# Softcap attention and a two-way maxout: six subtractions of the weights on one engine, and a new order of all work

## The chip, the cores and the metric

The kernel runs on one core of one Trainium2 chip. A core has a matrix engine (TensorE, PE in the profile; its weight loads are PEld), a vector engine (VectorE, DVE), a scalar engine for tanh and exp (ScalarE, ACT), a general engine (GpSimd, POOL) and a queue engine (SyncE, SP). Each takes its own instructions in order. Transfers between the outer memory and the core run on 16 DMA engines and are issued from the queues of POOL, SP and ACT. The metric is the time of one execution on the device, in microseconds (us), as the median over several runs: 332.95 us before the change (three runs, 332.04 to 333.63). All times within an execution count from the start of the span.

## What is computed

Attention over 8 batches of 12 heads, 448 positions and 64 channels, with a soft cap on the scores; its output, as 3584 rows of 768, goes through two weight matrices, an elementwise maximum and an output matrix:

```python
scores = scale * np.matmul(q, k.transpose(0, 1, 3, 2))
scores = cap * np.tanh(scores / cap)
attn = np.exp(scores - max); attn = attn / (sum + 1e-09)
x = np.matmul(attn, v)            # heads side by side: 3584 x 768
g = np.maximum(x @ w1, x @ w2)    # w1, w2: 768 x 1024
out = g @ w_out                   # 1024 x 768
```

(The lines are shortened from the reference.) Inputs and output are float32.

## The kernel before

**The second part, rewritten.** Since max(a, b) = relu(a - b) + b, the kernel computes out = relu(x (w1 - w2)) w_out + x (w2 w_out). Two things are made once at the start: `wd_sb` = w1 - w2, in six chunks c = 0..5 of 128 rows, and `wm_sb` = w2 w_out. The first needs one subtraction for each chunk: a float32 chunk of w1 (512 KB) and a bf16 chunk of w2, 128 partitions by 1024, written as bf16:

```python
def subtract(c, eng):
    eng.tensor_sub(wd_sb[:, c, :], w1_in[c], w2b[:, c, :])
```

`eng` is DVE or POOL. For `wm_sb` TensorE turns each w2 chunk (`W`, then `WC` copies it out), multiplies it with w_out in two halves of 8 matmuls (`P`; `OP` opens the PSUM bank) and DVE keeps the result (`PC`, line 389), which frees the bank.

**Staging of the weights.** The w2 chunks lie in the memory that later holds gT; w1 chunks 0 to 3 lie in the four output buffers `osb`, 4 and 5 in a buffer of `xT`. All these loads (`lw1`, `lw2`, `lwo`) and all loads of k, q and v (`lk`, `lq`, `lv`) are issued from POOL's queue, in order. A load into a buffer waits until its last readers are through.

**The first part.** It runs over 48 pairs of heads i, two of which make a tile t (24 tiles). For i < 10 TensorE turns q and k (`X i bank`, 28 small matmuls; DVE copies them out with `XC`); for later tiles an SP transpose by DMA does it (`cr t`). `S i j` are the scores of key chunk j (3 chunks of 128 keys), `T` their tanh and `E` their exp on ACT; `L`, `TL`, `EL` do the same for the last 64 keys of a tile. `A` and `B` add exps on DVE (for t >= 3), `Y` sums them on TensorE, `Y1` to `Y3` turn, invert and spread the sums on DVE. `VL` and `V` multiply with v, and `N t u` normalizes on DVE into `xT`. Scores and values share two PSUM tiles, `s0` and `s1`: a step that opens one of them waits for the one that read it last (`S 7 2`, for instance, waits for both `N 2`). DVE does `N t 1` in two instructions of half the partitions.

**The second part's main loop.** 120 groups: per batch 8 of x (w1 - w2) (columns 448 wide) and 6 or 8 of the output (384 wide). `M x y n` issues n pairs of half-array matmuls, the upper half of the rows for group x beside the lower half for group y; -1 means no partner, and `M x x` uses the whole array. `O` opens a PSUM bank, `H` and `Hs` hand a bank's accumulation from one half to the other over a marker instruction on DVE or SP, `ev` (DVE) or `eva` (ACT) evacuates, `st` stores by SP.

**What sets the order.** Nothing in the program chooses an order: the string `ORDER` (lines 9 to 166) lists every step of the whole kernel, and the steps are called in turn. Each step appends its instructions to the queue of its engine; engines run on their own and wait for one another by semaphores. So two steps of different engines may swap places in the string without effect, while two of the same engine change that engine's queue. Warm-up matmuls without use (`D`) keep TensorE busy in the beginning. The lines of the profile: `subtract` 354, `keep_wm` 389, `transposes` 410, `keep_warm` 423, `scores` 466, `tanh` 471, `left` 480, `ex` 488, `add` 500 and 505, `total` 518 to 525, `invert` 530 to 536, `values_left` 552, `values` 558, `normalize` 570 and 573, pairs of the main loop 597 (592 for the whole array), evacuation 622, 656, 658 and 661.

In the order before, POOL has `sub 5 1` (the 1 means POOL) between `lv 3 0` and `lv 3 1`; the other five are on DVE as 0, 2, 1, 3, 4.

Of the kernel before, what the change touches and what calls it, by code (L numbers as in the profile page):

```python
# [9 lines left out]
ld0 k; ld0 q; ms0; dm; cd k; lk 1 0; lq 1 0; lw2 3; lk 2 0; lw2 2; id; lq 3 0; lq 2 0; lw2 0; lw2 1; lk 3 0;  # L10
D 3 16; cd q; D 3 15; Xh 0 0 0; Xh 0 1; D 3 4; XCh 0 0; XCh 0 1; D 3 4; S 0 0; D 3 5; S 0 1; D 3 4; T 0 0; T 0 1;
D 3 4; S 0 2; D 3 12; X 1 1; D 3 16; W 3 2; XC 1; ms; WC 3; L 0; T 0 2; E 0 0 3; TL 0; S 1 2; D 3 8; X 2 2; S 1 0;
D 3 8; W 2 0; D 3 4; T 1 2; T 1 0; S 1 1; E 1 2 3; T 1 1; XC 2; S 2 1; D 3 1; W 1 3; X 3 2; S 2 0; W 0 1; lk 4 0;
lq 4 0; lwo 0 0; lwo 0 1; lv 0 0; lv 0 1; lk 6 0; lwo 1 0; lwo 1 1; lq 5 0; lv 1 1; lk 7 0; lq 6 0; lk 5 0; lw2 5;
lq 7 0; lv 1 0; T 2 1; T 2 0; WC 1; XC 3; WC 2; WC 0; L 1; X 4 2; S 2 2; OP 2 0 0; P 2 0 1; OP 1 0 1; P 1 0 3;
OP 0 0 3; P 0 0 2; P 1 0 1; P 0 0 1; P 2 0 1; P 0 0 1; P 2 0 2; P 1 0 1; P 2 0 3; P 1 0 3; P 2 0 1; TL 1; EL 0;
T 2 2; EL 1; E 1 0 2; XC 4; PC 2 0; PC 1 0; S 3 0; VL 0; V 0 1 0 2; Y 0 0; V 0 0 0 3; V 0 1 2 3; Y1 0; Y2 0; Y3 0;
N 0 1; N 0 0; T 3 0; E 2 0 3; S 3 1; OP 2 1 2; P 2 1 2; OP 1 1 0; P 1 1 1; OP 0 1 1; P 0 1 1; P 0 0 1; P 1 1 2;
P 0 1 3; P 0 0 2; P 2 1 2; P 1 1 1; P 0 0 1; S 3 2; T 3 1; E 3 0 2; T 3 2; S 4 0; P 0 1 2; P 1 1 2; P 0 1 2;
P 2 1 3; P 1 1 1; S 4 1; T 4 0; E 3 2 3; T 4 1; PC 0 1; PC 0 0; S 4 2; X 5 1; OP 3 0 3; P 3 0 2; P 2 1 1; P 1 1 1;  # L20
XC 5; PC 2 1; PC 1 1; L 2; W 5 1; T 4 2; TL 2; VL 1; V 1 0 0 1; Y 1 0; V 1 0 1 3; V 1 1 0 3; S 5 0; Y1 1; Y2 1;
WC 5; Y3 1; lv 2 1; lw2 4; lk 8 0; lq 9 0; lq 8 0; lw1 0; lw1 2; lk 9 0; lv 2 0; E 4 0 3; T 5 0; X 6 0; XC 6;
N 1 0; N 1 1; P 3 0 3; S 5 1; OP 3 1 2; P 3 1 1; W 4 0; P 3 0 3; P 3 1 7; S 5 2; EL 2; T 5 1; E 5 0 2; T 5 2;
WC 4; PC 3 1; PC 3 0; sub 0 0; S 6 0; OP 4 0 0; P 4 0 8; X 7 3; S 6 1; PC 4 0; XC 7; sub 2 0; T 6 0; E 5 2 3;
T 6 1; S 6 2; X 8 2; X 9 0; L 3; T 6 2; TL 3; Y 2 3; VL 2; S 7 0; V 2 1 0 1; EL 3; T 7 0; XC 8; XC 9; Y1 2; lw1 1;
lw1 5; lk 10 1; lw1 3; lw1 4; lk 12 1; lk 10 0; lq 11 0; lv 3 0; sub 5 1; lv 3 1; lk 11 0; lk 11 1; lq 10 0;
V 2 1 1 2; V 2 0 0 3; V 2 1 2 3; OP 5 0 3; P 5 0 1; OP 4 1 0; P 4 1 2; OP 5 1 2; P 5 1 1; S 7 1; P 4 1 2; P 5 1 3;
P 4 1 1; P 5 1 1; P 5 0 4; P 4 1 1; P 5 0 3; P 5 1 3; P 4 1 2; E 6 0 3; T 7 1; Y2 2; Y3 2; sub 1 0; N 2 1; N 2 0;
sub 3 0; PC 5 0; PC 5 1; sub 4 0; S 7 2; S 8 0; E 7 0 2; T 7 2; T 8 0; O 0 1; M 0 -1 1; O 1 3; M 1 -1 2; M 0 -1 3;
S 8 1; M 0 -1 2; M 1 -1 1; S 8 2; Hs 0; cr 5; T 8 1; T 8 2; E 7 2 3; M 1 0 3; O 2 2; M 2 0 3; L 4; VL 3; A 3 1 1;  # L30
A 3 0 1; A 3 0 2; B 3 0; B 3 1; PC 4 1; A 3 1 2; TL 4; V 3 0 0 3; V 3 1 0 3; Y 3 0; S 9 0; M 2 1 3; ev 0; Y1 3;
Hs 2; EL 4; T 9 0; E 8 0 3; O 3 0; M 3 1 3; M 3 2 3; Hs 3; lv 4 1; lv 4 0; lq 12 0; lv 5 0; lk 13 0; lk 13 1;
lk 12 0; lq 13 0; lk 15 0; lv 6 3; lv 5 2; lk 14 1; lk 15 1; lq 14 0; lk 14 0; lv 5 3; lq 15 0; lv 5 1; S 9 1;
O 4 1; M 4 2 3; M 4 3 3; Y2 3; Y3 3; ev 1; N 3 0; ev 2; T 9 1; Hs 4; O 5 3; M 5 3 3; M 5 4 3; O 6 2; M 6 4 3;
ev 3; N 3 1; A 4 0 1; ev 4; Hs 5; M 6 5 3; O 7 0; M 7 5 2; S 10 0; Hs 6; M 7 5 1; M 7 6 1; S 9 2; M 7 6 2; Hs 7;
cr 6; E 9 0 2; T 10 0; T 9 2; E 9 2 3; O 8 1; M 8 6 3; S 10 2; M 8 7 3; S 10 1; A 4 1 1; ev 5; A 4 0 2; H 8;
B 4 1; B 4 0; A 4 1 2; ev 6; T 10 1; T 10 2; O 9 3; M 9 7 3; M 9 8 5; L 5; M 9 8 2; VL 4; V 4 1 0 2; Y 4 2;
V 4 0 0 3; V 4 1 2 3; TL 5; E 10 0 3; ev 7; Y1 4; Y2 4; Y3 4; N 4 1; N 4 0; S 11 0; M 9 8 4; O 10 0; M 10 8 3;
Hs 9; Hs 8 2; T 11 0; EL 5; M 10 9 3; M 8 9 2; S 11 1; M 8 9 4; S 11 2; M 8 9 2; O 11 2; M 11 9 1; T 11 1; T 11 2;
E 11 0 2; M 11 9 2; S 12 0; M 11 10 5; S 12 1; M 11 10 6; T 12 1; T 12 0; E 11 2 3; A 5 0 1; ev 8; O 12 1;  # L40
M 12 10 3; cr 7; Hs 11; H 10 2; A 5 1 1; ev 9; A 5 0 2; B 5 1; B 5 0; M 12 11 3; M 10 11 1; L 6; M 10 11 2;
S 12 2; M 10 11 5; ev 10; A 5 1 2; TL 6; T 12 2; O 13 3; M 13 11 3; S 13 0; M 13 12 4; VL 5; Y 5 0; V 5 1 0 3;
V 5 0 0 3; T 13 0; E 12 0 3; M 13 12 4; S 13 1; M 13 12 3; lv 6 0; lk 17 0; lv 6 1; lk 16 0; lk 17 1; lv 7 0;
lv 7 3; lq 16 0; lq 17 0; lk 16 1; lk 19 1; lv 6 2; Y1 5; Y2 5; Y3 5; N 5 0; N 5 1; ev 11; T 13 1; EL 6; E 13 0 2;
Hs 13; O 14 0; M 14 12 3; M 14 13 1; S 14 0; M 14 13 2; Hs 12 2; Hs 14; S 13 2; M 12 13 8; O 15 2; M 15 13 3;
# [12 lines left out]
S 18 0; M 24 25 4; O 27 2; M 27 25 3; M 27 26 5; S 18 1; T 18 0; E 17 2 3; T 18 1; M 27 26 1; S 18 2; M 27 26 5;
L 9; A 8 0 1; A 8 0 2; ev 24; A 8 1 1; B 8 1; B 8 0; A 8 1 2; ev 25; T 18 2; TL 9; O 28 1; M 28 26 3; VL 8;
V 8 0 0 1; Y 8 3; V 8 1 0 3; V 8 0 1 3; S 19 0; M 28 27 3; E 18 0 3; T 19 0; Y1 8; cr 10; st 1 3; Hs 26 2; Hs 28;  # L60
M 26 27 8; O 29 3; M 29 27 3; S 19 1; EL 9; T 19 1; Y2 8; Y3 8; N 8 0; N 8 1; A 9 0 1; ev 26; A 9 0 2; ev 27;
S 19 2; M 29 28 8; S 20 0; M 29 28 3; O 30 0; M 30 28 3; Hs 29; Hs 28 2; lk 23 0; lk 22 0; lq 23 0; lk 23 1;
lk 22 1; lq 22 0; lv 9 3; lv 9 1; M 30 29 3; T 19 2; E 19 0 2; T 20 0; E 19 2 3; Hs 30; cr 11; M 28 29 8; S 20 1;
O 31 2; M 31 29 3; S 20 2; M 31 30 3; A 9 1 1; B 9 1; ev 28; ev 29; B 9 0; H 31; A 9 1 2; T 20 1; T 20 2; O 32 1;
M 32 30 3; M 32 31 3; Y 9 3; L 10; VL 9; V 9 1 0 2; V 9 0 0 3; V 9 1 2 3; E 20 0 3; TL 10; ev 30; Y1 9; Y2 9;
Y3 9; st 1 6; Hs 32; O 33 0; M 33 31 3; M 33 32 2; S 21 0; M 33 32 1; O 34 3; M 34 32 3; EL 10; T 21 0; N 9 0;
N 9 1; ev 31; ev 32; Hs 33; lk 25 0; lq 25 0; lv 10 0; lv 10 1; lk 25 1; lk 24 1; lv 11 0; lk 24 0; lq 24 0;
lv 10 2; lv 10 3; lk 26 1; lv 11 3; S 21 2; M 34 33 3; S 21 1; O 35 2; M 35 33 3; Hs 34; st 1 5; T 21 2; T 21 1;
E 21 0 2; M 35 34 3; Hs 35; O 36 1; M 36 34 3; M 36 35 3; S 22 1; S 22 0; ev 33; ev 34; A 10 0 1; A 10 0 2; Hs 36;
# [665 lines left out]
```

## Time and profile before

| | |
|---|---|
| median of three runs | 332.95 us (332.04 to 333.63) |
| the profiled execution | 335.05 us, its span 333.3 us |
| mean granted TensorE clock | 0.992 |
| TensorE busy | 325.7 us (98%) |
| ScalarE busy | 284.4 us (85%) |
| VectorE busy | 240.1 us (72%) |
| GpSimd busy | 164.8 us (49%) |
| TensorE's share of the chain that ended last | 84% |
| subtractions (line 354) on VectorE, of 1.21 to 3.17 us | 5 |
| subtraction on GpSimd, 2.14 us | 1 |

The page gives for each engine the busy time and its share of the span, a strip of 40 slices (each 8.3 us) with the busy share in tenths, and the chain: the work that ended last, followed back step by step to what released it. Rows of instructions name a line, an engine, an operation, and the tile written from the tile read. A row of waits says who waited for whom, with the total, the number of times and the longest. Busy time on TensorE counts from a matmul's start to its modelled end; pairs on the two halves of the array overlap, so sums of durations exceed the time.

### The profile page before, as it was taken

How to read it: one execution, taken by the hardware profiler on the slowest of the kernel's cores; microseconds unless marked ns; L12 is line 12 of the kernel's file. 1: busy time of each engine (PE TensorE's matmuls, PEld its weight loads, DVE VectorE, ACT ScalarE, POOL GpSimd, SP SyncE). 2: the span in 40 equal slices, each digit the busy share in tenths (PEclk: the TensorE clock that was granted, in tenths of full speed). 3: DMA queues.
4: the chain of work that ended last, by engine and by line, in shares of the span. 5: the costliest groups of instructions: out<-in, count | busy, mean ns of one | idle time of the engine just before them, and what ended most of it. 6: DMA issues, size and time to landing. Idle time of an engine off the chain costs nothing.

```text
span 333.3 us, 9760 instructions
## 1 busy us (share of the span) xinstructions
PE 325.7 (98%) x4137; PEld 189.2 (57%) x4139; DVE 240.1 (72%) x421; ACT 284.4 (85%) x276; POOL 164.8 (49%) x240
## 2 busy tenths in 40 slices
PE   8999998999999999999999999999999999999995
PEld 3555552555656555555655565555465555557872
DVE  1346899796886887877897769968897878973201
ACT  3999996999999999999999999999999999941120
POOL 7655583762665960685595566393717532000000
PEclk9999997999999999999999999999999999999998
DMA  8999999899799999999999989699989999100136
GB/s 134 203 201 190 221 265 144 65 132 115 61 151 181 141 182 156 148 133 149 155 132 166 138 140 163 155 136 138 182 115 96 143 137 185 38 2 2 47 96 190
DMA packets 134507, 46.05 MB, mean 138 GB/s; under 512 B 112320, under 2 KB 129472, under 8 KB 134464
## 3 DMA queue, kind: packets, MB, share of 16 engines
q0 software_dynamic: 94880, 25.25, 75.6%
q1 hardware_dynamic: 39280, 19.77, 26.9%
q8 instruction: 32, 0.52, 0.6%
q10 hardware_dynamic: 304, 0.43, 0.4%
q14 instruction: 11, 0.09, 0.1%
HBM read 47.78 MB, written 11.01 MB: 176 GB/s over the span
## 4 chain that ended last, share of the span: by engine, by line
PE 84%; DVE 8%; DMA 3%; ACT 2%; issue 1%; POOL 0%; DVEq 0%
PE mm L597 56%; PE s L558 8%; PE s L466 7%; DMA osb<-in_moe_w_dram 3%; PE mm L383 3%; PE s L480 2%; DVE gT L622 2%; PE s L552 2%; PE mm L525 2%; DVE xT L573 1%; PE mm L592 1%; PE mm L423 1%; ACT e L471 1%; PE mm L410 1%; DVE esum L500 1%
## 5 line engine op out<-in xcount | busy, mean ns | idle before, releaser
L471 ACT ACTIVATE e<-s 128x896 bf16<-128x896 f32 x144 | 127.1, 916 | 8.7 <-PE s L466 6.8
L488 ACT ACTIVATE e<-e 128x1792 bf16<-128x1792 bf16 (+2 forms) x72 | 122.2, 1698 | 0.7
L597 PE MATMUL mm<-wo_sb,gT 64*128 64x384 bf16 x864 | 115.6, 323 | 0.0
L597 PE MATMUL mm<-wm_sb,xT 64*128 64x384 bf16 x648 | 103.6, 323 | 0.2
L597 PE MATMUL mm<-xT,wd_sb 64*128 64x448 bf16 x768 | 100.9, 353 | 1.3 <-DVE wm_sb L389 0.9
L597 PEld LDWEIGHTS <-gT 64*128 64x128 bf16 x864 | 59.1, 94 | 25.7 <-issue 2.3
L597 PEld LDWEIGHTS <-wd_sb 64*128 64x128 bf16 x768 | 50.1, 95 | 29.4 <-issue 5.2
L292 POOL DMA_DIRECT2D kqs<-in_k_dram x76 | 54.7, 723 | 13.2 <-DMA qkT<-kqs 10.2
L597 PEld LDWEIGHTS <-xT 64*128 64x128 bf16 x648 | 49.9, 94 | 19.8 <-issue 3.1
L466 PE MATMUL s<-qkT 64*128 64x448 bf16 x288 | 53.4, 353 | 0.5 <-DVE xT L570 0.4
L316 POOL DMA_DIRECT2D vp<-in_v_dram x48 | 30.7, 642 | 44.8 <-PE s L558 20.8
L622 DVE TENSOR_SCALAR gT<-mm 128x448 bf16<-128x448 f32 x64 | 38.7, 618 | 12.1 <-PE mm L597 11.7
L316 POOL DMA_DIRECT2D vl<-in_v_dram x38 | 23.6, 623 | 34.7 <-PE s L552 29.7
L292 POOL DMA_DIRECT2D kqs<-in_q_dram x38 | 35.3, 929 | 6.4 <-issue 6.4
L558 PE MATMUL s<-e,vp 128*32 128x448 bf16 x576 | 35.4, 354 | 0.0
L658 DVE COPY osb<-mm 128x384 f32<-128x384 f32 x44 | 23.9, 555 | 14.5 <-PE mm L597 13.7
L573 DVE TENSOR_TENSOR xT<-s,inv 64x448 bf16<-64x448 f32 x48 | 29.9, 622 | 1.4
L500 DVE TENSOR_TENSOR esum<-e 128x896 bf16<-128x896 bf16 x42 | 25.6, 616 | 6.6 <-PE mm L597 4.0
L500 DVE TENSOR_TENSOR esum<-esum,e 128x896 bf16<-128x896 bf16 x42 | 26.1, 623 | 3.0 <-PE s L466 0.6
L505 DVE TENSOR_TENSOR esum<-esum,el 64x896 bf16<-64x896 bf16 x42 | 26.0, 619 | 2.4 <-PE mm L597 1.3
L656 ACT COPY osb<-mm 128x384 f32<-128x384 f32 x10 | 4.8, 479 | 26.0 <-PE mm L597 25.7
L466 PEld LDWEIGHTS <-qkT 64*128 64x128 bf16 x288 | 17.0, 94 | 17.1 <-issue 6.8
(57 smaller groups left out, 268.6 us busy)
## 6 DMA issues: line engine op xcount, KB each, us to landing
out_dram<-osb SPq DMA_DIRECT2D x54, 192.0 KB, 3.4
vp<-in_v_dram POOLq DMA_DIRECT2D x38, 160.0 KB, 4.1
kqs<-in_q_dram POOLq DMA_DIRECT2D x47, 112.0 KB, 4.4
kqs<-in_k_dram POOLq DMA_DIRECT2D x76, 56.0 KB, 3.9
osb<-in_moe_w_dram POOLq DMA_DIRECT2D x4, 512.0 KB, 9.4
gT<-in_moe_w_dram POOLq DMA_DIRECT2D x6, 256.0 KB, 6.7
wo_sb<-in_moe_w_out_dram POOLq DMA_DIRECT2D x4, 384.0 KB, 8.4
vp<-in_v_dram POOLq DMA_DIRECT2D x10, 128.0 KB, 5.6
```

Source lines behind the costliest of these rows:

```text
L292: nc.gpsimd.dma_start(out=to, in_=x)
L316: nc.gpsimd.dma_start(out=to, in_=x)
L466: scored[i, j] = nc.tensor.matmul(s[:, h, :S], k_of(t, o, h, j), q_of(t, o, h)).ins
L471: nc.scalar.activation(expo[i][:, 2 * j : 2 * j + 2, :], slots[i, j][:, :, :S], AF.Tanh, scale=scale / cap)
L488: nc.scalar.activation(e, e, AF.Exp, scale=float(cap))
L500: nc.vector.tensor_add(d, e[:, 0:2, :] if j == 1 else d, e[:, 2 * j : 2 * j + 2, :])
L505: nc.vector.tensor_add(d, d, left_e[t][r, :, :])
L558: nc.tensor.matmul(vals[t][place(m, u), u, :S], w[:, m, :], expo[2 * t + o][:, 2 * j + h, :], start=False, stop=(j == NJ - 1))
L573: nc.vector.tensor_mul(x[64 - r : 128 - r], vals[t][r : r + 64, u, :S], sums[t, 3][64 - r : 128 - r])
L597: ins = nc.tensor.matmul(self.ps, w[r], x[r], start=first, stop=self.at == [self.n, self.n]).ins
L622: nc.vector.tensor_relu(gT[b // 2][:, f, cs], ps)
L658: nc.vector.tensor_copy(o[:, hs], ps)
```

## The change

Only the string `ORDER` changes. The six subtractions all run on VectorE, in the order 0, 2, 1, 4, 3, 5, and POOL has none. All lists are new: the order of loads in POOL's queue, of matmuls, of DVE's and ACT's work and of SP's markers, stores and transposes. The steps are the same ones, with some of them cut differently (a run of `P`, `V` or `M` may be split by other work at another place). In the part that builds the weights:

```diff
-ld0 k; ld0 q; ms0; dm; cd k; lk 1 0; lq 1 0; lw2 3; lk 2 0; lw2 2; id; lq 3 0; lq 2 0; lw2 0; lw2 1; lk 3 0;
-D 3 16; cd q; D 3 15; Xh 0 0 0; Xh 0 1; D 3 4; XCh 0 0; XCh 0 1; D 3 4; S 0 0; D 3 5; S 0 1; D 3 4; T 0 0; T 0 1;
...
-XC 5; PC 2 1; PC 1 1; L 2; W 5 1; T 4 2; TL 2; VL 1; V 1 0 0 1; Y 1 0; V 1 0 1 3; V 1 1 0 3; S 5 0; Y1 1; Y2 1;
-WC 5; Y3 1; lv 2 1; lw2 4; lk 8 0; lq 9 0; lq 8 0; lw1 0; lw1 2; lk 9 0; lv 2 0; E 4 0 3; T 5 0; X 6 0; XC 6;
-N 1 0; N 1 1; P 3 0 3; S 5 1; OP 3 1 2; P 3 1 1; W 4 0; P 3 0 3; P 3 1 7; S 5 2; EL 2; T 5 1; E 5 0 2; T 5 2;
-WC 4; PC 3 1; PC 3 0; sub 0 0; S 6 0; OP 4 0 0; P 4 0 8; X 7 3; S 6 1; PC 4 0; XC 7; sub 2 0; T 6 0; E 5 2 3;
-T 6 1; S 6 2; X 8 2; X 9 0; L 3; T 6 2; TL 3; Y 2 3; VL 2; S 7 0; V 2 1 0 1; EL 3; T 7 0; XC 8; XC 9; Y1 2; lw1 1;
-lw1 5; lk 10 1; lw1 3; lw1 4; lk 12 1; lk 10 0; lq 11 0; lv 3 0; sub 5 1; lv 3 1; lk 11 0; lk 11 1; lq 10 0;
-V 2 1 1 2; V 2 0 0 3; V 2 1 2 3; OP 5 0 3; P 5 0 1; OP 4 1 0; P 4 1 2; OP 5 1 2; P 5 1 1; S 7 1; P 4 1 2; P 5 1 3;
-P 4 1 1; P 5 1 1; P 5 0 4; P 4 1 1; P 5 0 3; P 5 1 3; P 4 1 2; E 6 0 3; T 7 1; Y2 2; Y3 2; sub 1 0; N 2 1; N 2 0;
-sub 3 0; PC 5 0; PC 5 1; sub 4 0; S 7 2; S 8 0; E 7 0 2; T 7 2; T 8 0; O 0 1; M 0 -1 1; O 1 3; M 1 -1 2; M 0 -1 3;
-S 8 1; M 0 -1 2; M 1 -1 1; S 8 2; Hs 0; cr 5; T 8 1; T 8 2; E 7 2 3; M 1 0 3; O 2 2; M 2 0 3; L 4; VL 3; A 3 1 1;
-A 3 0 1; A 3 0 2; B 3 0; B 3 1; PC 4 1; A 3 1 2; TL 4; V 3 0 0 3; V 3 1 0 3; Y 3 0; S 9 0; M 2 1 3; ev 0; Y1 3;
...
+ld0 k; ld0 q; dm; ms0; cd k; id; lq 2 0; lk 1 0; lq 1 0; lw2 3; lq 3 0; lw2 0; lw2 2; lk 2 0; lw2 1; lk 3 0;
+lwo 0 0; D 3 16; cd q; D 3 15; Xh 0 0 0; Xh 0 1; XCh 0 1; XCh 0 0; D 3 12; S 0 0; D 3 5; S 0 1; T 0 0; T 0 1;
...
+P 3 0 2; W 5 1; S 5 0; Y1 1; Y2 1; Y3 1; WC 5; lw2 4; lq 8 0; lk 7 0; lk 8 0; lw1 0; lq 9 0; lw1 2; lq 7 0; lw1 1;
+lk 9 0; lv 2 0; lv 2 1; E 4 0 3; T 5 0; V 1 1 1 3; X 6 0; N 1 0; XC 6; N 1 1; P 3 0 1; OP 3 1 2; P 3 1 2; S 5 1;
+P 3 1 1; P 3 0 1; P 3 1 1; W 4 0; P 3 1 4; P 3 0 4; S 5 2; EL 2; T 5 1; E 5 0 2; T 5 2; WC 4; sub 0 0; PC 3 1;
+PC 3 0; S 6 0; OP 4 0 0; P 4 0 8; S 6 1; X 7 3; sub 2 0; PC 4 0; XC 7; T 6 0; E 5 2 3; T 6 1; X 8 2; S 6 2; O 0 1;
+M 0 -1 1; L 3; T 6 2; TL 3; Y 2 3; X 9 0; S 7 0; VL 2; EL 3; T 7 0; E 6 0 3; XC 8; sub 1 0; Y1 2; XC 9; Y2 2;
+Y3 2; lw1 4; lw1 3; lk 11 0; lw1 5; lv 3 0; lv 3 1; lk 10 1; lk 11 1; lq 10 0; lq 11 0; lk 10 0; V 2 1 0 1;
+V 2 0 0 3; V 2 1 1 3; OP 5 0 3; P 5 0 2; OP 4 1 0; P 4 1 1; OP 5 1 2; P 5 1 2; P 4 1 1; P 5 1 1; S 7 1; P 5 0 2;
+P 5 1 2; P 4 1 5; P 5 0 4; T 7 1; E 7 0 2; sub 4 0; N 2 0; N 2 1; A 3 0 1; sub 3 0; PC 5 0; sub 5 0; S 8 0; S 7 2;
+M 0 -1 1; P 4 1 1; P 5 1 3; O 1 3; M 1 -1 1; T 7 2; T 8 0; S 8 1; M 0 -1 3; S 8 2; M 0 -1 1; M 1 -1 2; Hs 0; cr 5;
+T 8 1; T 8 2; E 7 2 3; M 1 0 3; L 4; VL 3; V 3 0 0 1; V 3 1 0 2; V 3 0 1 3; V 3 1 2 3; A 3 0 2; A 3 1 1; PC 4 1;
+B 3 0; B 3 1; A 3 1 2; PC 5 1; TL 4; Y 3 0; S 9 0; O 2 2; M 2 0 3; M 2 1 3; Y1 3; Y2 3; ev 0; Y3 3; Hs 2; E 8 0 3;
...
```

Behind this the main loop keeps its pairs, its banks and its markers; what changes is where the first part's steps stand between them. Two examples, each from the same place of both orders:

```diff
-M 9 7 3; M 9 8 5; L 5; M 9 8 2; VL 4; V 4 1 0 2; Y 4 2; V 4 0 0 3; V 4 1 2 3; TL 5;
+M 9 7 3; M 9 8 3; L 5; VL 4; V 4 1 0 1; V 4 0 0 2; Y 4 2; V 4 0 2 3; V 4 1 1 3; TL 5;
...
-M 32 30 3; M 32 31 3; Y 9 3; L 10; VL 9; V 9 1 0 2; V 9 0 0 3; V 9 1 2 3;
+M 32 30 3; L 10; VL 9; V 9 1 0 1; Y 9 3; V 9 0 0 3; V 9 1 1 3; M 32 31 3;
```

## The prediction

> **What bounds the kernel now.** I read the page first: busy shares, then the strip of the granted clock, then the chain; after that the windows, the waits and the timeline where the strip has its dent.
>
> ```profile
> PE 325.7 (98%) x4137; PEld 189.2 (57%) x4139; DVE 240.1 (72%) x421; ACT 284.4 (85%) x276; POOL 164.8 (49%) x240
> ...
> PEclk9999997999999999999999999999999999999998
> ...
> PE 84%; DVE 8%; DMA 3%; ACT 2%; issue 1%; POOL 0%; DVEq 0%
> ```
>
> TensorE (PE) carries 84% of the chain and is busy 98%. Both orders issue the same matmuls: counted in the two lists, 1131 paired steps, 28 whole and 18 single ones in the second part, 96 products P, and warm-up of 101 units. So only time in which PE waits, runs at a cut clock, or changes between shapes can be won or lost. The 7 in the clock strip is the seventh slice, 50 to 58 us. The windows there (us of the stretch, then busy us and instructions of each engine, clock, DMA, GB/s) and the waits from 46 to 62 us:
>
> ```profile
> 48.08:51.50 3.42, 3.01 (x21) 1.62 (x20) 3.38 (x5) 3.25 (x3) 3.42 (x6) 1.00 1.29 110
> 51.50:54.91 3.41, 2.24 (x16) 0.86 (x12) 3.41 (x6) 2.51 (x3) 1.75 (x3) 1.00 1.44 130
> 54.91:58.33 3.42, 3.42 (x31) 1.06 (x28) 3.28 (x6) 1.89 (x3) 0.00 (x0) 0.50 1.01 161
> ```
>
> ```profile
> PE mm L597 <- DVE wm_sb L389: 0.9, 1, 0.9
> ...
> PE s L466 <- DVE xT L570: 0.4, 1, 0.4
> PE mm L597 <- DVE wd_sb L354: 0.3, 1, 0.3
> ```
>
> VectorE (DVE) is busy in all of 48.08 to 54.91; PE waits for it three times, is busy 2.24 of 3.41 us (66%), and in the 3.41 us behind that its clock is 0.50. What holds DVE, from the timeline (start, us, engine):
>
> ```profile
> 40.21 1.21 DVE L354 TENSOR_TENSOR wd_sb<-osb,gT 128x1024 bf16<-128x1024 f32 x1
> ...
> 45.99 2.14 POOL L354 TENSOR_TENSOR wd_sb<-xT,gT 128x1024 bf16<-128x1024 f32 x1
> 46.05 3.17 DVE L354 TENSOR_TENSOR wd_sb<-osb,gT 128x1024 bf16<-128x1024 f32 x1
> ...
> 51.06 1.22 DVE L354 TENSOR_TENSOR wd_sb<-osb,gT 128x1024 bf16<-128x1024 f32 x1
> ```
>
> The subtraction on GpSimd (POOL) ends at 48.13. The DVE one that began beside it took 3.17 us where the others took 1.21 to 1.22, and ends at 49.22, 1.09 us after POOL's: as if it had stood still until POOL was done.
>
> **The change part by part.** *sub 5 leaves POOL.* DVE's sub 1 falls from 3.17 to 1.22: 1.95 us less. POOL loses 2.14 us, in front of lv 3 1 and the loads of tile 5, which cr 5 on SP's queue waits for; cr 5's transpose is first read by S 10 0 at 65.88, some 7 us after it landed, so this earns nothing.
>
> *sub 5 comes to DVE:* one more 1.22 us, placed behind PC 5 0. Net on DVE 0.73 us less. Bounds: nothing less if sub 1 was slow for another reason (then 1.22 more), 1.95 less if the new one fell into idle time; DVE is dense from 38.6 to 58.6, so I take the sum.
>
> *The start.* The identity (id, 0.43 us) moves from fifth to first place in POOL's queue and waits there for DVE's second memset, so all loads shift by about 0.5 us. Ahead of S 0 0 stand 43 instead of 39 units of warm-up; 4 units took 0.43 us at the cold clock (3.49 us for 31). The warm memset comes first, some 0.1 us earlier. S 0 0 and with it ScalarE (ACT), dense from 7.14 to 51.37, starts about 0.3 us later. Bounds 0 and 0.5.
>
> *The dense stretch.* DVE's work from WC 4 (38.62) to A 3 1 2 (58.59) is 19.97 us; minus 0.73, plus the 0.3 of the start, it ends at about 58.15. Its last piece is now PC 5 1 (0.5), so A 3 1 2 ends near 57.7 and Y 3 0, which sums its result, can run at 57.7 instead of 59.66. Behind it PE has S 9 0 (0.2) and M 2 0 3 (0.56), which stood before L 4 until now: done near 58.9, against 60.15 for the same work. That is 1.2 us won at full clock.
>
> *What PE waits for then.* S 8 0 now stands before S 7 2, which needs N 2's bank; N 2 ends near 50.8 (51.13 before). P 4 1 1 and P 5 1 3 (4 x 0.163) fill PE to about 51.5. Then M 1 -1 1 waits for bank 3, that is for PC 5 0, now behind A 3 0 1 and sub 3: near 53.1 (52.7 before). Queued behind it on PE are S 8 1, M 0 -1 3 and S 8 2; ACT waits for S 8 1 under 1 us, as now (0.80). The next M 0 -1 1 waits for sub 5, near 54.3. So PE idles 1.6 us in one piece and some 0.8 us in others: its busy share between 51.5 and 54.9 would be about half, below the 66% that stood before the cut. Only two other windows were followed by a cut or a cold clock: the start and the end; the next higher share, 88% (48.08 to 51.50), was not. So I expect the cut again. 3.4 us at half clock do 1.7 us of the 2.9 us of work up to Y 3 0, PE ends that near 59.0 and, after S 9 0, M 2 0 3 near 59.85: of 1.2 us 0.3 stay.
>
> The Trainium skill, "TensorE: Matmul & The Clock Gate", Part 1 and its closing table, has the clock fall after an idle window of about 3.4 us. Here it fell with no PE wait over 0.86 us, so the rule taken at its word differs from this trace. By it the changed kernel would keep its clock and the 1.2 us whole.
>
> *Loads of w1.* The order is now lw1 0, lq 9, lw1 2, lq 7, lw1 1, lk 9, lv 2 0, lv 2 1, lw1 4, lw1 3, lk 11 0, lw1 5. No more than eight POOL loads are out at once: lw1 4 was issued 2.39 us late at 39.96, just after lw1 0 had landed (39.67 by its landing marks). The DMA is backlogged from 4 us on, so bytes decide. By the end of the last w1 both orders have moved the same number: 48.5 us before; 0.5 later by the start, 0.5 earlier since lw1 0 no longer stands behind lq 9, which waited for X 5 until 31.49. Needed near 53: covered. But lq 7, which landed at 30.47, now stands behind two w1. Before, two w1 and a k load landed 7.4 us after the load ahead of them (35.03 to 42.44). Now the load ahead lands near 33.4, so lq 7 lands near 41.4 with lq 9 between; X 7 3, in PE's queue behind S 6 1, would run at 41.4 to 41.8. ACT needs S 6 2, two transposes later, near 43.3: cost 0 to 0.3; I take 0.1. The bounds: a w1 took 1.25 us in the backlog's best part and 4.6 at worst, so lq 7 lands from 36.5 to 43.9 and costs 0 to 2.6.
>
> *The rest, 60 to 333 us.* Same groups, banks and handshakes (107 by SP, 22 by DVE). I compared starts of neighbouring PE steps with the work between. A change from M to L costs 0.19 us in the median, from M to VL, V to M or V to S 0.105; L straight to VL gives 0.11 back; M to S and back costs nothing. Counted in the two lists: M to L 17 to 19, L to VL 9 to 13, M to VL 11 to 7, V to M 11 to 8, V to S 5 to 9, Y to L (0.32) 1 to 0. That is 0.38 - 0.44 - 0.42 - 0.32 + 0.42 - 0.32, about 0.7 less; seven single changes of other kinds take some of it back (0 to 0.5). I take 0.4 less, bounds 0.8 less and 0. Waits there: three stretches where the chain runs on DVE (95 to 101, 199 to 208, 236 to 244 us) cost 0.4 to 0.9 each by the same comparison; they may move. The last v load lands 0.1 to 4 us before VL reads it in 11 of 19 tiles; in the new list it stands as far ahead of VL or further, so I cost this at nothing. If one missed by 1 us, PE would stand 1 us.
>
> *Sum:* -0.3 (dense stretch, with the clock cut) - 0.4 (shape changes) + 0.1 (X 7 3) = -0.6 us. The profiled execution took 335.05 us (span 333.3 and 1.75 around it), 2.1 above the median of 332.95; the sum gives 334.45 for it and 332.3 for the median. About 0.5% (1.7 us) is what a measurement of this kernel can tell from no change.
>
> **The rivals.**
> - *The clock stays whole.* For it: the 88% window passed, and where the 3.4 us windows fall against the waits may differ from run to run. Against: half-busy PE. -1.2 - 0.4, and 0.2 more if ACT's late start is absorbed: 331.2. If every loss in 50 to 58 us went (4.6 us by the same comparison of starts), it would be 328.3; DVE's dense stretch excludes that.
> - *lq 7 arrives late (slower).* One transpose stops PE, then ACT and all behind. For it: the two slowest w1 loads stand just ahead of it. Against: bytes give 41.4. At the slow bound +2.6 - 0.6: 334.9. It decides from a landing near 43.6 us on.
> - *The long sub was not POOL's doing,* and sub 1 stays at 3.17: 1.95 later, 334.2. Against: it ended just one normal duration after POOL's.
> - *New pile-ups on DVE after 60 us,* as the three above, two or three more of 0.4 to 0.9 us: +2 - 0.6, 334.4, up to 335.5. For it: all lists are new. Against: the same groups in the same banks.
>
> The Trainium skill, "SBUF — State Buffer", on the port pair that DVE and GpSimd share, says that a DVE op with two SBUF inputs blocks a GpSimd op that reads SBUF, and that DVE's two-port copies keep POOL from writing DMA descriptors. Strictly read, each further DVE subtraction could hold POOL's issues up to 1.2 us. The rows deny it here: beside the sub at 51.06 two issues took 1.26 us, 0.63 each, as elsewhere.
>
> **How the numbers follow.** Forecast 0.36 (332.3, its own range 331.3 to 333.5; 0.06 faster, 0.27 same, 0.03 slower); whole clock 0.28 (0.20 faster, 0.08 same); late lq 7 0.16 (0.05 same, 0.11 slower); long sub 0.05 (0.03 same, 0.02 slower); pile-ups 0.15 (0.05 same, 0.10 slower). Faster 0.26, same 0.48, slower 0.26. The range reaches into the whole-clock case to 330.4 and into the late load and the pile-ups to 335.4.
>
> **What would show it.** Six L354 rows on DVE of 1.2 us each, none on POOL; sub 5 ending near 54.3; A 3 1 2 near 57.7; a PE wait for wm_sb L389 of 1.3 to 1.7 us; the clock at 0.50 in one window after it; X 7 3 at 41.4 to 41.8; M 2 0 3 ending near 60 (59 with a whole clock). The forecast is wrong if POOL's row was not what slowed sub 1, if PE waits for a transpose near 41 us, or if PE's waits after 60 us differ by more than 1 us.

## The result, and the profile after

The changed kernel took 332.38 us (median of 20 runs, 331.68 to 334.02), the kernel before 334.27 us beside it (20 runs, 331.78 to 336.22): a ratio of 0.9949, 95% interval 0.9927 to 0.9971. The forecast's 332.3 stands beside 332.38, but by luck, since two errors cancel: the median of the three runs shown before lies 1.3 us below the 334.27 of all twenty, of which they are the first, and the gain is 1.9 us where 0.6 were forecast. The interval lies below 1; the prediction had put 0.26 on a gain that can be told from no change, and 0.48 on none.

The fastest runs of both kernels lie 0.1 us apart. What differs is the rest. Of all 133 runs of the kernel before that were made for this document (331.78 to 337.23, median 334.30), 84 took over 334 us; of the 28 of the changed kernel, one did (334.02). Two runs of b_pool_late (336.76 and 338.08 us), over 1.5% above the fastest of their kernel, count as a slower state of the chip and are left out below. So the question is which losses came in most runs of the one and hardly in the other.

The page of the changed kernel's profiled execution (332.29 us, span 330.5): engines, strip of the granted clock, chain.

```profile
PE 322.7 (98%) x4137; PEld 187.0 (57%) x4139; DVE 239.4 (72%) x422; ACT 284.0 (86%) x276; POOL 162.6 (49%) x239
...
PEclk9999999999999999999999999999999999999999
...
PE 88%; ACT 4%; DMA 4%; DVE 1%; POOL 0%; issue 0%; SPq 0%; DVEq 0%
```

DVE is down from 8% of the chain to 1%, and the dent in the clock strip is gone. The windows from 48.08 to 58.33 us (busy us and instructions of PE, PEld, DVE, ACT, POOL; clock, DMA, GB/s):

```profile
48.08:51.50 3.42, 3.42 (x22) 1.60 (x22) 3.36 (x6) 3.39 (x4) 1.06 (x2) 1.00 1.49 95
51.50:54.91 3.41, 3.41 (x37) 1.61 (x35) 3.41 (x6) 3.41 (x6) 0.00 (x0) 1.00 0.00 0
54.91:58.33 3.42, 3.42 (x60) 1.57 (x49) 3.25 (x7) 3.42 (x3) 1.57 (x3) 1.00 0.68 142
```

PE is busy in all of them, where it was at 3.01 and 2.24 before the 0.50 window. DVE is as dense as before, but PE no longer waits for it. The timeline of DVE there:

```profile
46.74 1.18 DVE L354 TENSOR_TENSOR wd_sb<-xT,gT 128x1024 bf16<-128x1024 f32 x1
...
50.18 1.21 DVE L354 TENSOR_TENSOR wd_sb<-osb,gT 128x1024 bf16<-128x1024 f32 x1
51.42 0.56 DVE L389 CAST wm_sb<-mm 128x384 bf16<-128x384 f32 x1
51.90 1.22 DVE L354 TENSOR_TENSOR wd_sb<-xT,gT 128x1024 bf16<-128x1024 f32 x1
...
55.93 0.62 DVE L500 TENSOR_TENSOR esum<-esum,e 128x896 bf16<-128x896 bf16 x1
```

The six subtractions take 1.18 to 1.22 us each. Sub 5, the last, ends at 53.12; `A 3 1 2` at 56.55; `M 2 0 3`, the last of the work compared in the prediction, begins at 57.11 and is done near 57.7, where the same work was done at 60.15. So 2.4 us of the profile's 2.76 are won in this stretch. From 62 us on the view lists no PE wait, as it listed none in the profile of before.

The loads of w1, in the page's rows of DMA issues (KB each, median us from issue to landing), first before, then after:

```profile
osb<-in_moe_w_dram POOLq DMA_DIRECT2D x4, 512.0 KB, 9.4
```

```profile
osb<-in_moe_w_dram POOLq DMA_DIRECT2D x4, 512.0 KB, 6.5
```

They land 2.9 us sooner after their issue; the last w1 chunk landed at 48.53 us before and at 46.29 after.

### The profile page after: what moved, and what is told of

It is laid out like the page before. It is cut to its first block, busy times and chain, and to the rows that moved or that the text cites. A ratio compares the mean times of both kernels' runs of the same rounds, so it can differ in the third digit from the quotient of the medians.

```text
span 330.5 us, 9759 instructions
## 1 busy us (share of the span) xinstructions
PE 322.7 (98%) x4137; PEld 187.0 (57%) x4139; DVE 239.4 (72%) x422; ACT 284.0 (86%) x276; POOL 162.6 (49%) x239
## 2 busy tenths in 40 slices
DMA packets 134507, 46.05 MB, mean 139 GB/s; under 512 B 112320, under 2 KB 129472, under 8 KB 134464
## 4 chain that ended last, share of the span: by engine, by line
PE 88%; ACT 4%; DMA 4%; DVE 1%; POOL 0%; issue 0%; SPq 0%; DVEq 0%
PE mm L597 60%; PE s L558 8%; PE s L466 8%; PE mm L383 3%; DMA wo_sb<-in_moe_w_out_dram 3%; ACT e L471 2%; PE s L480 2%; PE mm L525 2%; ACT e L488 2%; PE s L552 2%; PE mm L592 1%; DMA kqs<-in_q_dram 1%; DVE xT L573 0%; PE mm L518 0%; PE mm L410 0%
## 5 line engine op out<-in xcount | busy, mean ns | idle before, releaser
L488 ACT ACTIVATE e<-e 128x2688 bf16<-128x2688 bf16 (+2 forms) x72 | 122.1, 1699 | 0.8
L597 PE MATMUL mm<-xT,wd_sb 64*128 64x448 bf16 x768 | 99.1, 349 | 0.1
L597 PEld LDWEIGHTS <-wd_sb 64*128 64x128 bf16 x768 | 48.9, 94 | 28.3 <-issue 2.5
L558 PE MATMUL s<-e,vp 128*32 128x448 bf16 x576 | 34.7, 354 | 0.0
```

The lines of the kernel that those rows point to most:

```text
L488: nc.scalar.activation(e, e, AF.Exp, scale=float(cap))
L558: nc.tensor.matmul(vals[t][place(m, u), u, :S], w[:, m, :], expo[2 * t + o][:, 2 * j + h, :], start=False, stop=(j == NJ - 1))
L597: ins = nc.tensor.matmul(self.ps, w[r], x[r], start=first, stop=self.at == [self.n, self.n]).ins
```

## The experiments

Theory at the start: the long subtraction, sub 1 beside POOL's sub 5, is the whole gain. Rivals: the new order is the gain; the clock's cut is; a v load is. Medians are of runs made beside the kernel before on the same chip; the ratio is worked out from all runs of the two kernels and need not be that of the two medians; the last column counts runs over 334 us. Three kernels' strings fill five lines less, so their line numbers are 5 lower (`b_again`, `b_sub5_dve`, `a_sub5_pool`); in `a_then_b` they are 76 higher.

| kernel | median us | before, us | ratio (95%) | over 334 |
|---|---|---|---|---|
| b_again | 334.23 | 333.99 | 1.0004 (0.9978 to 1.003) | 7 of 12 |
| b_sub5_dve | 333.97 | 333.99 | 0.9997 (0.997 to 1.0025) | 6 of 12 |
| a_sub5_pool | 333.30 | 333.99 | 0.9996 (0.9959 to 1.0032) | 4 of 12 |
| a_then_b | 334.52 | 333.99 | 1.0033 (1.0012 to 1.0054) | 11 of 12 |
| a_again | 332.30 | 334.68 | 0.9942 (0.9915 to 0.997) | 0 of 8 |
| b_pool_late | 333.43 | 334.68 | 0.9969 (0.994 to 0.9998) | 3 of 10 |
| b_pool1_first | 334.64 | 334.68 | 0.9995 (0.9967 to 1.0024) | 8 of 12 |
| b_pool1_late | 335.33 | 334.68 | 1.0021 (0.9994 to 1.0048) | 9 of 12 |
| b_v15 | 333.54 | 334.46 | 0.9975 (0.995 to 0.9999) | 5 of 12 |
| b_v15_late | 333.28 | 334.46 | 1.0002 (0.997 to 1.0033) | 4 of 12 |
| b_v15_dve | 333.25 | 334.46 | 0.9969 (0.9945 to 0.9994) | 4 of 12 |
| a_v15_late | 335.54 | 334.46 | 1.0046 (1.002 to 1.0072) | 12 of 12 |

**b_again: the kernel before once more**, nothing edited.

> The kernel before, unchanged, once more: its second profile and the granted clock of each timed run. If the cut of the clock behind the waits at 51 to 55 us belongs to the order, every run shows a mean clock near 0.992 (3.4 us at half of 333), and the profile again has a DVE subtraction of about 3.2 us beside POOL's, PE waits of 1 to 2 us there and the 0.50 window. If these hang on when the w1 loads land, the runs fall into two kinds, near 331.8 us with clock 1.0 and near 334 us with 0.99, and the stretched DVE instruction is another one, or none, in this profile. If the difference of the two orders is nothing but the drift of single runs, the median lies near 332.4.

Its profile has a span of 330.4 us, no more than the changed kernel's 330.5. The timeline of the subtractions in it:

```profile
46.08 3.21 POOL L349 TENSOR_TENSOR wd_sb<-xT,gT 128x1024 bf16<-128x1024 f32 x1 [0.29 <-DMA xT<-in_moe_w_dram]
46.11 1.18 DVE L349 TENSOR_TENSOR wd_sb<-osb,gT 128x1024 bf16<-128x1024 f32 x1
```

Here POOL waits and DVE does not. Before, POOL began 0.06 us ahead (45.99 and 46.05) and DVE took 3.17; here POOL's row begins 0.03 ahead, takes 3.21 instead of 2.14, and DVE takes 1.18. So the kernel before holds a race of some tens of ns. Here POOL's start waited for w1 chunk 5, which landed at 46.01 (45.78 there). The difference between PE's starts in the two profiles is 0.19 to 0.21 us from `S 2 0` (16 us) to `S 7 1` (47 us). The lost race makes 1.58 of it by `S 8 2`, and with the cut of the clock it is 2.92 at `S 9 1`; behind that the two run side by side (`S 47 2` at 290.32 and 287.46, 2.86 apart). The windows of this profile show no cut:

```profile
48.08:51.50 3.42, 3.42 (x24) 1.79 (x22) 3.41 (x6) 3.39 (x4) 3.42 (x5) 1.00 0.85 79
51.50:54.91 3.41, 3.30 (x39) 1.79 (x37) 3.33 (x6) 3.41 (x5) 2.92 (x4) 1.00 1.47 120
```

How often the kernel before is cut can be told from the mean clocks, which are on record for 113 of its 133 runs. One stretch of 3.41 us at half clock takes 1.7 of 333 us, 0.5% off the mean. 26 runs have a mean of 0.995 or less, and their median is 335.46 us. The other 87 are too high for such a stretch, and their median is 334.06, still 1.7 us above the changed kernel's 332.38. So the cut makes runs long, but it is the smaller part of the difference between the two medians.

The Trainium skill, "SBUF — State Buffer", section "SBUF: two separate sides", calls the pair of ports that VectorE and GpSimd share an exclusive lock: whichever starts first holds it for its whole instruction and the other stands. The 3.17 and 3.21 us agree on the standing, in both directions; on who wins, the rows agree in one profile and are 0.03 us the other way in this one.

**b_sub5_dve: all six on DVE in the order before.**

```diff
-lq 11 0; lv 3 0; sub 5 1; lv 3 1;
+lq 11 0; lv 3 0; lv 3 1;
-PC 5 0; PC 5 1; sub 4 0; S 7 2;
+PC 5 0; PC 5 1; sub 4 0; sub 5 0; S 7 2;
```

> The order before, with sub 5 on VectorE right behind sub 4 and all else as it was. Theory of the shared hold (GpSimd's subtraction stops VectorE's): sub 1 takes 1.2 us instead of 3.2, N 2 ends near 49.2, the waits for N 2 and PC 5 go; sub 5 ends near 53.6 and PE waits for it about 1 us, and for the sums of tile 3 up to 1 us; whether the clock is cut is open. Ratio 0.994 to 0.998 to the kernel before. Rival, the order made the gain: 0.998 to 1.003, since VectorE has as much to do in the same stretch. Rival, POOL's subtraction was not the cause: sub 1 still takes about 3 us and the ratio is 1.003 or more.

No subtraction was long (1.18 to 1.22), and yet it was no faster than before. PE's waits from 44 to 62 us:

```profile
PE mm L592 <- DVE wd_sb L349: 0.8, 1, 0.8
PE mm L520 <- DVE esum L495: 0.3, 1, 0.3
```

PE now waits for the sixth subtraction. Its load is not late: its chunk landed at 45.58, and DVE, which waits for nothing here between 36 and 58 us, comes to it at 52.20. The race is gone, its price is not: taking the subtraction off POOL alone is no gain in the order before.

**a_sub5_pool: the new order with sub 5 on POOL**, behind `lv 3 0` as it was.

```diff
-lw1 5; lv 3 0; lv 3 1;
+lw1 5; lv 3 0; sub 5 1; lv 3 1;
-sub 3 0; PC 5 0; sub 5 0; S 8 0;
+sub 3 0; PC 5 0; S 8 0;
```

> The new order, with sub 5 back on GpSimd behind lv 3 0, all else as it is. Theory of the shared hold: POOL's subtraction begins when lw1 5 has landed (near 46.3 us) and the VectorE instruction with two SBUF inputs that runs then, sub 4 at 46.7, takes about 3 us instead of 1.2; VectorE saves 1.2 us later, so PE waits about 1 us near 50 and the ratio to the kernel before is 0.995 to 0.998, 0 to 0.3% worse than the new order (0.995). Rival, the order made the gain and the engine does not matter: 0.995 within 0.1% and no PE wait. If a POOL instruction ahead of the later loads mattered, cr 5 would land later than S 10 0 needs it; I expect over 4 us of room.

The race comes back with another chunk: the subtractions in the timeline, PE's waits from 44 to 62 us, and the window:

```profile
47.01 2.13 POOL L349 TENSOR_TENSOR wd_sb<-xT,gT 128x1024 bf16<-128x1024 f32 x1 [5.44 <-DMA xT<-in_moe_w_dram]
47.18 3.04 DVE L349 TENSOR_TENSOR wd_sb<-xT,gT 128x1024 bf16<-128x1024 f32 x1
```

```profile
PE mm L592 <- DVE wm_sb L384: 1.0, 1, 1.0
PE s L461 <- DVE xT L568: 0.6, 1, 0.6
```

```profile
51.50:54.91 3.41, 1.87 (x13) 0.79 (x13) 3.38 (x6) 2.20 (x3) 3.41 (x5) 1.00 1.44 98
54.91:58.33 3.42, 3.42 (x54) 1.72 (x55) 2.88 (x6) 3.42 (x5) 1.19 (x2) 1.00 1.74 131
```

This is the picture that the prediction drew for the changed kernel: PE waits for `PC 5 0` and is busy 1.87 of 3.41 us (55%). But the clock stays at 1.00 behind it. The ratio, 0.9996 with an interval of 0.4% to each side, cannot tell the expected loss of 0 to 0.3% against the changed kernel from no gain at all. Four of 12 runs took over 334 us, the longest 337.18 at a clock of 0.988.

**a_then_b: the new order up to `M 2 1 3`, the old one behind it** (the steps that neither half then has, and those that both have, are put right at the seam).

```diff
 S 9 0; O 2 2; M 2 0 3; M 2 1 3;
-Y1 3; Y2 3; ev 0; Y3 3; Hs 2; E 8 0 3; T 9 0;
+lk 12 1; ev 0; Y1 3; Hs 2; EL 4; T 9 0; E 8 0 3;
...
```

> The new order up to M 2 1 3 (some 59 us), then the steps that are left in the old order. If the gain is made in the stretch that builds the weights, this keeps it less the 0.4 us that I laid on fewer changes of matmul shape in the main loop: ratio 0.995 to 0.997, and M 2 1 3 ends near 58.3 us with the clock whole. If the gain is the main loop's, the ratio is 0.999 to 1.002.

Missed: it was slower than before. PE's waits from 44 us to the end:

```profile
PE s L634 <- DMA vp<-in_v_dram: 1.1, 1, 1.1
PE mm L673 <- DVE st L606: 0.7, 1, 0.7
```

0.7 us is lost at the seam (59 us), where the halves do not fit. The 1.1 us stands in tile 15, far from any edit, and shows a second loss. In the order before, POOL's queue has `lv 16 0; lq 37 0; lv 15 0`: the last v load of tile 15 stands behind `lv 16 0`, which waits for `V 14`. In seven profiles with this old main loop it landed between 2.0 us after and 0.3 us before `VL 15` began; in the new order, where it is issued 10 us earlier, it lands 8 us ahead (the tile's last load 7). The prediction costed all v loads at nothing.

**a_again: the changed kernel once more**, nothing edited.

> The changed kernel once more, on the chip and in the hours of the three runs that follow. It has no subtraction on POOL. If the order before loses by a race between two subtractions for one hold, this kernel has no such race: median 0.4 to 0.8% below the kernel before, and its runs lie closer together (the middle 80% within 1.2 us, against 3 us and more before). If the wide spread is the chip's and not the order's, it spreads as widely as the kernel before.

332.0 to 332.91 in all eight runs: the changed kernel has one kind of run where the kernel before has several.

**b_pool_late, b_pool1_first, b_pool1_late: the race decided beforehand.** In the first, sub 5 goes one place back on POOL, so that DVE's sub 1 begins first. In the other two POOL and DVE swap chunks, with POOL's ahead of `lv 3 0` (first) or behind `lv 3 1` (late).

```diff
-lv 3 0; sub 5 1; lv 3 1;
+lv 3 0; lv 3 1; sub 5 1;
```

```diff
-lv 3 0; sub 5 1; lv 3 1;
+sub 1 1; lv 3 0; lv 3 1;
-Y3 2; sub 1 0; N 2 1;
+Y3 2; sub 5 0; N 2 1;
```

> The order before with one swap on POOL's queue: sub 5 stands behind lv 3 1 instead of ahead of it, so POOL reaches it near 46.7 us, 0.6 us after VectorE has begun sub 1 (46.05 to 46.11 in both profiles). Theory of the race: VectorE always comes first, sub 1 takes 1.2 us, POOL's takes 2.7 to 3.3 with its waiting, and nothing waits for it; no PE wait over 0.4 us at 50 to 56 us, span near 330.5, ratio 0.993 to 0.996, as the changed kernel. Rival, the median's loss has another cause in the order: ratio 0.998 to 1.002. Rival, any subtraction on POOL costs: above 0.998 with a stretched VectorE row later (sub 3 near 49).

> The order before, but POOL has sub 1 (its w1 chunk lands at 44.5 to 44.7) ahead of lv 3 0, and VectorE has sub 5 where sub 1 stood. POOL starts near 45.3 and VectorE's subtraction near 46.1, so POOL is always first. Theory of the race: VectorE's row takes 2.4 to 2.7 us in every run (till POOL's end near 47.4, then 1.1 more), N 2 ends 1.3 us later than in the other order of the two, PE waits 0.5 to 1.5 us at 51 to 55; ratio 1.000 to 1.005 to the kernel before, since that one loses the race only in part of its runs. Rival (no shared hold): the row takes 1.2 us and the ratio is below 0.997.

> The control of the run before: the same exchange of chunks 1 and 5, but POOL's subtraction stands behind lv 3 1, so VectorE is first. Theory of the race: VectorE's row takes 1.2 us, span near 330.5 to 331, ratio 0.993 to 0.997, 0.5% or more below the run with POOL first. If the two differ by less than 0.2%, who is first does not matter to the time.

The subtractions in the timelines of the three, in that order:

```profile
46.34 1.18 DVE L354 TENSOR_TENSOR wd_sb<-osb,gT 128x1024 bf16<-128x1024 f32 x1
47.22 2.30 POOL L354 TENSOR_TENSOR wd_sb<-xT,gT 128x1024 bf16<-128x1024 f32 x1
```

```profile
44.67 2.15 POOL L354 TENSOR_TENSOR wd_sb<-osb,gT 128x1024 bf16<-128x1024 f32 x1
45.37 2.54 DVE L354 TENSOR_TENSOR wd_sb<-xT,gT 128x1024 bf16<-128x1024 f32 x1
```

```profile
45.75 1.18 DVE L354 TENSOR_TENSOR wd_sb<-xT,gT 128x1024 bf16<-128x1024 f32 x1
46.30 2.64 POOL L354 TENSOR_TENSOR wd_sb<-osb,gT 128x1024 bf16<-128x1024 f32 x1
```

Whoever is ahead by 0.5 us or more is undisturbed, and the other is stretched until the first is through: DVE's 2.54 us ends 1.09 us behind POOL's, as in the profile of before. This is so in every profile where the two met: a stretched DVE row ends 1.08 to 1.09 us behind POOL's (four profiles), a stretched POOL row 1.99 to 2.00 us behind DVE's (four), each nearly as long as it takes alone. The mechanism is shown. As an account of the medians it is not enough: with DVE first, the runs still spread from 331.71 to 336.39 and from 332.12 to 336.78. b_pool_late has a ratio of 0.9969, its interval just short of no change; b_pool1_late, expected 0.5% or more below b_pool1_first, is 0.2% above it and no faster than before. The wait for tile 15's v load was in all three (0.6, 1.6 and 0.4 us).

**b_v15, b_v15_late, b_v15_dve: tile 15's load moved ahead**, alone, then with POOL's subtraction later (as in b_pool_late), then with sub 5 on DVE (as in b_sub5_dve).

```diff
-lq 34 0; lv 15 3;
+lq 34 0; lv 15 3; lv 15 0;
-lk 37 1; lv 16 0; lq 37 0; lv 15 0;
+lk 37 1; lv 16 0; lq 37 0;
```

> The order before with one load moved: lv 15 0, that stood on POOL's queue behind lv 16 0 (which waits for V 14), goes ahead to stand behind lv 15 3, with nothing else changed. Theory A (two places make up the gain: the race of the two engines at 45 us, and tile 15's late v load): PE's wait for vp at 198-210 us (0.4 to 1.6 us in five profiles of the old main loop) is gone, lv 15 0 lands 5 us or more ahead of VL 15, and the median comes down by 0.4-0.8 us (ratio 0.9975-0.999), the spread of its runs staying wide since the race is left in. Rival B (the race is the whole gain): ratio 0.999-1.001. Rival C (the load was late but something else is late right behind it): the vp wait is gone, another of the same size stands within 5 us of it, ratio 1.0.

> The order before, with lv 15 0 moved ahead as in the run of that move alone, and POOL's sub 5 one place later behind lv 3 1, so that DVE's sub 1 begins first. Six subtractions are still split five to one. Theory A (two places): both losses are gone and it is as fast as the changed kernel within its interval, 331.8-332.8 us, ratio 0.993-0.996, with a narrow spread. Rival B (the rest of the new order, its shape changes and earlier loads, carries a part): 333-333.5 us, ratio 0.996-0.998, like the run with sub 5 later alone.

> The order before, with lv 15 0 moved ahead and sub 5 on DVE behind sub 4, as the change puts it: the change without its new order. Theory A (two places): no race and no late load, 332.0-332.8 us, ratio 0.993-0.996. Rival B (DVE's six subtractions one after another need the new order, which lands the w1 loads 3 us earlier): PE waits 0.5-1 us for PC 5 or wd at 52-56 us, as in the run with sub 5 on DVE alone, and it stays at 333-334 us, ratio 0.996-1.0.

The load now lands 13 to 14 us ahead of `VL 15`, and no wait for vp is left in any of the three. b_v15 came as the theory of two places has it (0.9975), its interval just short of no change. The other two did not reach the changed kernel: 333.28 and 333.25, what rival B of each expected. In b_v15_late eight runs took 332.59 to 333.89 and four 335.35 to 336.98, these four with mean clocks of 0.994 and 0.995. Its ratio, with 1 inside the interval, and its median do not point the same way. In b_v15_dve, whose profiled run (334.52) is one of its four long ones, PE's waits from 44 us on are

```profile
PE mm L597 <- DVE wd_sb L354: 0.8, 1, 0.8
PE mm L597 <- SPq L606: 0.4, 1, 0.4
PE mm L518 <- issue: 0.3, 1, 0.3
PE mm L525 <- DVE esum L500: 0.3, 1, 0.3
```

the same 0.8 us for the sixth subtraction as in b_sub5_dve. Its last w1 chunk landed at 49.83 us, its last subtraction ended at 54.2; in the changed kernel these are 46.29 and 53.12, and PE does not wait. Here too it is not the load of the sixth that DVE waits for (landed at 46.83, read at 53.03). What earlier loads give is the place of the others: in the changed kernel four of the six subtractions begin before the time at which their chunk had landed in the kernel before (sub 1 at 43.71 against 44.49). So six subtractions on DVE cost PE nothing only in the new order, and (a_sub5_pool) the new order needs them there. Whether it is by its loads, by DVE's order or by what PE does meanwhile, no run separates.

The profile of b_v15 happened on a lost race (POOL 45.68 with 2.14 us, DVE 45.78 with 3.13), and it has the cut. The windows, with bounds where its clock changes:

```profile
50.46:53.87 3.41, 2.04 (x13) 0.77 (x12) 3.41 (x5) 2.37 (x4) 2.48 (x4) 1.00 1.43 118
53.87:57.28 3.41, 3.21 (x16) 1.79 (x17) 3.30 (x7) 2.35 (x3) 0.00 (x0) 0.50 0.92 106
```

**a_v15_late: the late load put into the new order.**

```diff
-lk 35 1; lv 15 0; lv 15 3; lv 15 1;
+lk 35 1; lv 15 3; lv 15 1;
-lk 36 1; lq 36 0; lq 39 0;
+lk 36 1; lq 36 0; lv 15 0; lq 39 0;
```

> The changed kernel with lv 15 0 put back behind lq 36 0, issued near 196.5 us and so landing near 202.5 us, where VL 15 starts at 200.9: the late load of the old order made anew in the new one. Theory A (a late v load is paid in full, PE having nothing else): a PE wait for vp of 1-2 us near 201 us, and a median of 333.0-334.0 us, 0.8-1.6 us above the changed kernel's 332.3. Rival (PE's other tasks take the place, or it is made up for later): no more than 0.3 us, 332.3-332.6.

It did not test what it was made for. `lv 15 0` now stands in the list behind the steps that read it, so `V 15` multiplies with what the load of tile 13 left there, and the load waits for `V 15`, with POOL's queue behind it. `lv 16 0` then landed at 213.63 us (210.56 in a_again), with `VL 16` at 210.74. The wait has moved by one tile, and it serves as well. PE's wait, and the windows at it, again with the clock's bounds:

```profile
PE s L558 <- DMA vp<-in_v_dram: 2.7, 1, 2.7
```

```profile
210.80:214.21 3.41, 0.76 (x28) 0.34 (x16) 1.77 (x3) 3.21 (x2) 1.57 (x3) 1.00 1.26 129
214.21:217.62 3.41, 3.41 (x34) 1.38 (x28) 1.32 (x3) 0.30 (x2) 1.49 (x3) 0.50 1.21 254
```

Its runs fall in two groups: seven at clocks of 0.998 to 1.000, median 334.62, 2.3 above the changed kernel's 332.3; five at 0.992 to 0.994, median 336.72, 2.1 more. The profiled run, with the cut in its trace, is one of the five; means of 0.998 and more are too high for one. So a v load that is late is paid nearly in full, if the seven waited as long as the profiled run, and by the mean clocks the wait draws a cut in some executions and not in others. In a_again, too, `lv 16 0` lands only 0.1 us ahead of `VL 16`, and none of that kernel's runs shows a price for it.

## Why the prediction was right or wrong

- *Sub 5 leaves POOL.* Sized right for the profile shown (3.17 to 1.21), and the rival that the long sub was not POOL's doing has fallen. What was missed: the row is one side of a race. In b_again the same kernel had DVE's 1.18.
- *Sub 5 comes to DVE.* 1.22 forecast and measured. That it needs cover elsewhere only the runs showed: in the order before PE stands 0.8 us for it.
- *The start.* Wrong in sign, without effect: `S 0 0` began at 6.04 us (6.54 before), `S 2 0` 0.6 later, `WC 4` at 38.37 (38.62 before, 38.9 forecast).
- *The dense stretch.* `A 3 1 2` ended at 56.55 against 57.7: 0.55 us from the start's wrong sign, the rest from DVE's rows overlapping more (1.60 us in all against 1.25).
- *What PE waits for then.* This step failed. `N 2` ended at 49.73 (50.8 forecast) and `PC 5 0` at 51.98 (53.1), so `M 1 -1 1` ran at 52.10 without a wait. The 1.6 us of idle PE and the cut that I expected of them did not come, and the stretch won 2.4 us where 0.3 were forecast. The path was that of the rival with the whole clock, and went beyond its 1.2 us. The rule behind the step, that a lower busy share brings the cut, was wrong too: windows with PE at 66% (before) and 60% (b_v15) were followed by one, the window at 55% (a_sub5_pool) was not.
- *The Trainium skill's rule on the clock* ("TensorE: Matmul & The Clock Gate", Part 1, "What's actually happening") has a window of about 3.4 us that runs freely, without regard to the kernel. The traces agree with that: the clock first rises at 3.87 us in one profile of the changed kernel and at 6.98 in the other, and the three cuts begin 14, 14 and 61 times 3.413 us after that rise (before, b_v15, a_v15_late). That PE need not be idle for a whole window (its longest wait before the cut here is 0.9 us) does not agree with the closing table.
- *Loads of w1.* `X 7 3` began at 41.51, as forecast (41.4 to 41.8), and PE did not wait, but not for the reason given: `lq 7` landed at 37.96 instead of 41.4. I had let bytes decide and taken both orders to have moved the same number by 48 us. By the windows, 4.6 MB moved from 30 to 46 us (250, 319, 303 and 281 GB/s) against 4.0 MB before (177, 203, 253, 358). Why was not tried. It let sub 0, 2, 1 and 4 begin where they did.
- *The rest.* From the end of the work compared in the prediction to the end of the span, 272.8 and 272.3 us pass in two profiles of the changed kernel, 273.1 and 273.2 in two of the kernel before: 0.3 to 0.9 won, 0.4 forecast. That the shapes did it is argued, not shown. No new pile-up came.
- *The v loads, costed at nothing.* Wrong for tile 15: in the profile shown it landed as `VL 15` began and so cost nothing there; in kernels with that main loop it cost 0.4 to 1.6 us where it came later.

In sum: the profiled execution fell by 2.76 us against 0.6, nearly all of it in 46 to 60 us. Against the best kind of execution of the kernel before (b_again's span of 330.4) the change wins nothing: the work that is done at 57.7 in the changed kernel's profile (58.2 in a_again) is done there at 57.25. It wins by runs that it does not have. Of what makes those long, the profiles of the kernel before show the lost race (1.4 us, and 1.3 more with the cut). Tile 15's load cost PE 0.4 to 1.6 us in four profiles of kernels with the same main loop, but in neither of its own two. How the 1.9 us divide stays open: each removal alone ended within 0.4% of before, both together (b_v15_late) did not reach the changed kernel, and no trace was recorded of the long runs of b_pool_late and b_v15_late.

## What to carry to other kernels

Before pricing a row that is out of line with its siblings, look at a second execution: if two engines meet there within a few tens of ns, the kernel has two times there, and a change that only removes the meeting cannot better the best run. A load that lands within some tenths of a us of its reader in one profile is late in others, so price it by what it costs when late times how often that may be. And taking work from one engine earns little when the engine that gets it is as full: here five subtractions on VectorE with one on GpSimd, or six on VectorE, were worth the same until the whole order, loads included, was built around the six.

## What the runs showed of the hardware

- A subtraction on VectorE and one on GpSimd, both reading the core's memory, stand still for one another, whichever is behind: 3.17, 3.13, 3.04 and 2.54 us for VectorE's 1.2; 3.21, 2.64 and 2.30 us for GpSimd's 2.14. In eight profiles the one behind ends 1.08 to 1.09 us (VectorE) or 1.99 to 2.00 us (GpSimd) after the other's end. A head start of 0.03 us in the rows did not decide it.
- Each of the three cuts of the clock within a kernel lasted one stretch of 3.41 us at 0.50. The share of time in which PE was busy in the 3.41 us ahead does not decide alone: 66%, 60% and 22% were followed by a cut, 55% was not. What does was not tried; the uncut stretch held matmuls of the whole array, the one at 66% did not. One kernel with a wait of 2.7 us at the same place in its order has mean clocks of 0.992 to 0.994 in five of 12 runs and 0.998 to 1.000 in seven.
- Where no race and no cut interferes, an execution repeats closely: the starts of PE's steps in two executions were 2.92 us apart at 60 us and 2.86 apart at 290.
